# A two-byte shift in place for one of two three-operand instructions in a double-to-float weight conversion

## The chip, the cores and the metric

The kernel runs on one core of one Trainium2 chip. The metric is the device time of one execution in microseconds (us). The profile of one execution is shown beside it. Its engines are TensorE (PE, with its weight loads as PEld), VectorE (DVE), ScalarE (ACT), GpSimd (POOL) and SyncE (SP).

## The reference

Three blocks run one after another, for a batch of 2, 448 tokens and a width of 768:

```
scores = q @ k.T / 8, causal mask, softmax          # 12 heads of 64
x      = (softmax @ v), heads side by side
xk, xr = mu * x + (1 - mu) * x_prev                 # x_prev: the token before
x      = sigmoid(xr @ w_r) * (relu(xk @ w_k)^2 @ w_v)
h      = relu(x @ w_in)
c      = three-tap convolution of h along the tokens
out    = (h * sigmoid(c)) @ w_out
```

The weights `w_r` (768x768), `w_k` and `w_in` (768x1024), `w_v` and `w_out` (1024x768) and the taps `conv_w` reach the kernel as 64-bit floats, the rest as 32-bit floats.

## The kernel before

**Weights.** Each weight matrix is cut into slices: 6 of `w_r` (wr0 to wr5), 8 of `w_k` (wk), 6 of `w_v` (wv), 8 of `w_in` (wi) and 8 of `w_out` (wo). A slice is 128 partitions by 768 values, for wv 128 by 1024. Each is loaded as it is, eight bytes a value, into one of two `wraw` buffers, and `narrow` turns it into 32-bit floats in five steps:

- **a** on ACT: the absolute value of the upper four-byte words, read as floats (they are a double's sign, exponent and first 20 mantissa bits).
- **b** on DVE, or on POOL where the plan says `/p`: clamped to the range that a 32-bit float can hold.
- **c** on DVE: shifted left by 3, with a mask, which moves the exponent and the mantissa to their places.
- **d** on DVE, line 144: sign and top exponent bit are taken from the upper words and put in (three operands: upper words, constant, result so far).
- **e** on DVE, line 146: the top three bits of the lower words are put in as the last mantissa bits (three operands again).

After e the raw buffer is free for the next load. Then ACT makes the high half of a split of the slice (step h, line 87), and DVE or POOL the low half (step l, line 91). TensorE multiplies with both halves, in three passes (`mm3`, line 66). The same five steps run once on a small block of 24 by 128 values, the taps, at the start (`first_steps`).

**Order.** There are three stretches. Attention, the products with `w_r` and the first with `w_k` (up to about 125 us) follow a list written out by hand, `ORDER`, in which each token such as `w3:d` places one step on its engine's queue. The products with `w_k` and `w_v` (to about 238 us) are left to a planner that orders the instructions of each engine by simulated costs. The last stretch, with `w_in`, the convolution and `w_out`, follows a second written list, `LATE`. In each engine's queue instructions run in order. Loads of slices are on SP's queue, each behind step e of the slice that held its buffer.

Of the kernel before, what the change touches and what calls it, by code (L numbers as in the profile page):

```python
# [9 lines left out]
F32 = mybir.dt.float32  # L10
I32 = mybir.dt.int32
I64 = mybir.dt.int64
F32R = mybir.dt.float32r
AF = mybir.ActivationFunctionType
ALU = mybir.AluOpType
# [4 lines left out]
def kernel(  # L20
# [18 lines left out]
    nc = tc.nc  # L39
# [70 lines left out]

    raws = Slots(wp, "wraw", 2, [P, NF * P], I64)
    wcs = Slots(wp, "wc", 2, [P, NF * P])
    whls = Slots(wp, "whl", 4, [P, 2, NF * P], F32R)
    mslots = Slots(mixp, "m", 3, [P, 512])
# [3 lines left out]
    def in_order(ins):  # L118
        if pinned[0]:
            tc.keep_in_program_order(ins)  # L120
# [5 lines left out]
    def as_float(bits):  # L126
        return struct.unpack("<f", struct.pack("<I", bits))[0]

    def as_int(bits):
        return bits - (1 << 32) if bits >> 31 else bits  # L130

    def narrow(step, dst, raw, eng="v"):

        lo, hi = raw[:, 0::2], raw[:, 1::2]
        d = dst.bitcast(I32)
        if step == "a":
            in_order(nc.scalar.activation(dst, hi.bitcast(F32), AF.Abs))
        elif step == "b":
            e = nc.gpsimd if eng == "p" else nc.vector
            e.tensor_scalar(dst, dst, as_float(HIGH), as_float(LOW), ALU.min, ALU.max)  # L140
        elif step == "c":
            nc.vector.tensor_scalar(d, d, 3, as_int(0x3FFFFFF8), ALU.logical_shift_left, ALU.bitwise_and)
        elif step == "d":
            nc.vector.scalar_tensor_tensor(d, hi, as_int(0xC0000000), d, ALU.bitwise_and, ALU.bitwise_or)
        else:
            nc.vector.scalar_tensor_tensor(d, lo, 29, d, ALU.logical_shift_right, ALU.bitwise_or)

    def load(w, m, name, rows, raw=None):

# [17 lines left out]
    def convert(raw, n, name, c=None):  # L167

        c = wcs.turn(f"{name}c") if c is None else c
        for s in "abcde":  # L170
            narrow(s, c[:, :n], raw.bitcast(I32)[:, :2 * n])
        return c
# [30 lines left out]
    def home(tag):  # L203
        return act if tag in early else late[0]

    def big(tag, name):
        return home(tag).tile([P, 2, NT], F32R, tag=tag, name=name)

# [240 lines left out]
    def slot(dtype, name):  # L449
        tag = wo_slots.pop(0)  # L450
        return home(tag).tile([P, 2, WT], dtype, tag=tag, name=name)
# [3 lines left out]
    def first_steps(s):  # L455

        if s == "L":
            t = act.tile([P, 4 * P], F32, tag="U2", name="small")
            small["m"] = mr = t[:2 * NC, :P]
            in_order(nc.sync.dma_start(out=mr[:NC], in_=mu_k.rearrange("(c p) -> c p", p=P)))  # L460
            in_order(nc.sync.dma_start(out=mr[NC:], in_=mu_r.rearrange("(c p) -> c p", p=P)))
            small["r"] = cr = t[:3 * NF, 2 * P:]
            in_order(nc.gpsimd.dma_start(out=cr.bitcast(I64), in_=conv_w.rearrange("t (f p) -> (t f) p", p=P)))
            small["c"] = t[:3 * NF, P:2 * P]
        elif s in "an":
            for x in "a" if s == "a" else "bcde":
                narrow(x, small["c"], small["r"].bitcast(I32))
        elif s == "T":
            pm = bank("small", 1)
            nc.tensor.transpose(pm[:, :2 * NC], small["m"], ident[:2 * NC, :2 * NC])  # L470
            nc.tensor.transpose(pm[:, P:P + 3 * NF], small["c"], ident[:3 * NF, :3 * NF])
        else:
            pm = used("small")
            nc.vector.tensor_copy(mu[:, :2 * NC], pm[:, :2 * NC])
            nc.vector.tensor_scalar(mu[:, 2 * NC:4 * NC], mu[:, :2 * NC], -1.0, 1.0, ALU.mult, ALU.add)
            nc.vector.tensor_copy(cw, pm[:, P:P + 3 * NF])

    class Slice:
# [3 lines left out]
        def step(self, s, eng):  # L482
            e, n = self.e, NC * P
            if s == "L":
                self.raw = raws.get(e, f"{self.name}{self.m}raw")
                load(self.w, self.m, self.name, False, self.raw)
            elif s in "abcde":
                if s == "a":
                    self.c = wcs.get(e, f"{self.name}{self.m}c")
                narrow(s, self.c[:, :n], self.raw.bitcast(I32)[:, :2 * n], eng or "v")  # L490
                if s == "e":
                    raws.put(e)
            elif s == "h":
                self.t = whls.get(e, f"{self.name}{self.m}hl")
                split_h("s", self.t[:, 0, :n], self.c[:, :n])
            else:
                split_l(eng or "v", self.t[:, 1, :n], self.c[:, :n], self.t[:, 0, :n])
                wcs.put(e)
# [143 lines left out]
    def convert_next():  # L642
# [10 lines left out]
        if i < KH:  # L653
            t = slot(F32R, f"b11_{i}")
        wo_c.append(c := convert(*x, slot(F32, f"wo{i}c").rearrange("p a b -> p (a b)")))
# [206 lines left out]
    def pair(name):  # L862
        x = pairs.pop(0)
        if isinstance(x, tuple):
            e, i = x
            if e not in st:
                st[e] = late[0].tile([P, 2, 2, WT], F32R, tag=f"X{e}", name=f"st{e}")
            x = st[e][:, i]
# [195 lines left out]
```

## Time and profile before

| what | value |
|---|---|
| time, median of 3 runs | 354.03 us (353.97 to 354.67) |
| span of the profiled execution | 351.6 us |
| busy PE / DVE / ACT / POOL | 345.2 / 306.9 / 235.1 / 90.3 us |
| granted TensorE clock, mean | 1.000 |

The span runs from the first to the last instruction of the profiled execution; 354.03 - 351.6 = 2.43 us of the median lie around it, and the profiled execution's own time is taken as its span and these 2.43 us. A busy share is an average over the stretches, which have different limits, so what a change is worth is read from who waits for whom.

### The profile page before, as it was taken

The page shows a single profiled execution, that of the slowest core. Times are in us where ns is not written, and L with a number is a line of the kernel's source. Part 1 is how long each engine was busy: PE and PEld are TensorE (multiplying, and loading weights), DVE is VectorE, ACT ScalarE, POOL GpSimd, SP SyncE. Part 2 cuts the span into 40 slices and gives each one's busy share as a digit, 9 for nine tenths or more (in the row PEclk, how much of TensorE's full clock was granted, in tenths as well). Part 3 has the DMA queues.
Part 4 walks back from the last instruction along what each step waited for, and adds up shares of the span by engine and source line. Part 5 has one row for each costly group of instructions (what it writes and reads, how often), then busy time and mean ns, then how long its engine had stood idle before and what let it go on. Part 6 is the DMA issues. An engine that isn't in the chain of part 4 may idle for free.

```text
span 351.6 us, 7196 instructions
## 1 busy us (share of the span) xinstructions
PE 345.2 (98%) x2682; PEld 309.2 (88%) x2682; DVE 306.9 (87%) x629; ACT 235.1 (67%) x515; POOL 90.3 (26%) x149
## 2 busy tenths in 40 slices
PE   7999999999999999999999999999999999999996
PEld 7678788888999998998889999988988999999995
DVE  2999999999889878989999998997998999897741
ACT  2999999999533276767786464354756877766501
POOL 3386986667435000000000000000000000368100
PEclk9999999999999999999999999999999999999999
DMA  5686597442033155347455434543232200379623
GB/s 132 146 222 144 127 222 213 90 116 93 7 95 106 66 180 181 121 148 240 142 187 171 156 101 173 179 143 128 89 103 79 89 2 0 67 134 202 138 91 135
DMA packets 63228, 45.33 MB, mean 129 GB/s; under 512 B 34752, under 2 KB 62156, under 8 KB 63192
## 3 DMA queue, kind: packets, MB, share of 16 engines
q1 hardware_dynamic: 59352, 40.68, 38.7%
q0 software_dynamic: 2912, 3.96, 6.6%
q8 instruction: 21, 0.34, 0.4%
q10 hardware_dynamic: 928, 0.23, 0.3%
q14 instruction: 15, 0.12, 0.1%
HBM read 38.17 MB, written 2.75 MB: 116 GB/s over the span
## 4 chain that ended last, share of the span: by engine, by line
PE 95%; DVE 1%; DMA 1%; POOL 1%; SPq 1%; issue 1%; ACT 0%; POOLq 0%
PE pk L66 17%; PE pv L66 17%; PE pr L66 13%; PE A L66 7%; PE po L391 6%; PE s L321 4%; PE B L66 4%; PE c L66 2%; PE Yb L363 2%; PE D L66 2%; PE Xa L363 2%; PE W L561 1%; PE q L300 1%; PE ph5l L66 1%; PE ph6l L66 1%; PE ph4l L66 1%
## 5 line engine op out<-in xcount | busy, mean ns | idle before, releaser
L887 POOL DMA_DIRECT2D s<-g x12 | 12.7, 1177 | 194.9 <-ACT st L87 188.6
L343 ACT ACTIVATE p<-e,st 128x448 f32<-128x448 f32 (+6 forms) x84 | 42.1, 507 | 1.7 <-DVE st L334 1.5
L72 POOL TENSOR_SCALAR p<-p,st 128x64 f32<-128x64 f32 (+6 forms) x70 | 34.6, 512 | 20.7 <-DVE st L334 11.4
L334 DVE CUSTOM_DVE_ANT_0 e<-s,mask 128x192 f32<-128x192 f32 (+6 forms) x84 | 31.6, 415 | 0.4 <-ACT p L343 0.2
L391 PE MATMUL po<-pt,v 128*64 128x128 f32 (+4 forms) x384 | 24.0, 277 | 0.0
L807 DVE SCALAR_TENSOR_TENSOR cv<-hT,cw,cv 128x448 f32<-128x448 f32 x32 | 21.5, 681 | 2.7 <-ACT cv L804 2.6
L391 PEld LDWEIGHTS po<-pt,v 128*64 128x64 f32 x384 | 20.0, 137 | 3.3 <-issue 0.3
L321 PE MATMUL s<-kT,qT 64*64 64x384 f32 (+6 forms) x336 | 22.1, 386 | 0.5 <-DVE kT L79 0.2
L321 PEld LDWEIGHTS s<-kT,qT 64*64 64x64 f32 x336 | 14.9, 132 | 6.6 <-ACT qT L79 0.7
L343 ACT ACTIVATION_READ_ACCUMULATOR p<-e,st 128x1 f32 x84 | 16.3, 194 | 0.0
L91 POOL TENSOR_TENSOR xr<-m,xr 128x448 fp32r<-128x448 f32 x10 | 12.0, 1198 | 2.1 <-ACT xr L87 1.7
L87 ACT ACTIVATE x<-xv 128x512 fp32r<-128x512 f32 (+1 forms) x12 | 6.8, 573 | 8.1 <-DVE xv L706 8.0
L811 ACT ACTIVATE cv<-cv 128x448 f32<-128x448 f32 x16 | 9.1, 571 | 3.2 <-DVE cv L807 3.2
L999 ACT ACTIVATE o<-A 128x384 f32<-128x384 f32 x3 | 1.5, 491 | 14.7 <-PE A L66 14.6
L804 ACT ACTIVATE cv<-hT,cw 128x448 f32<-128x448 f32 x16 | 10.7, 668 | 0.5 <-DVE g L91 0.3
L813 DVE TENSOR_TENSOR cv<-cv,hT 128x448 f32<-128x448 f32 x16 | 9.9, 621 | 1.2 <-ACT cv L811 1.2
L91 DVE TENSOR_TENSOR k<-a,k 128x512 fp32r<-128x512 f32 (+2 forms) x16 | 9.9, 619 | 0.0
L66 PE MATMUL pv<-k,wv0hl 128*128 128x512 f32 (+1 forms) x48 | 9.9, 364 | 0.0
L66 PE MATMUL pv<-k,wv4hl 128*128 128x512 f32 (+1 forms) x48 | 9.8, 363 | 0.0
L66 PE MATMUL pv<-k,wv2hl 128*128 128x512 f32 (+1 forms) x48 | 9.8, 363 | 0.0
L66 PE MATMUL pv<-k,wv3hl 128*128 128x512 f32 (+1 forms) x48 | 9.8, 363 | 0.0
L66 PE MATMUL pv<-k,wv5hl 128*128 128x512 f32 (+1 forms) x48 | 9.8, 363 | 0.0
(516 smaller groups left out, 1105.0 us busy)
## 6 DMA issues: line engine op xcount, KB each, us to landing
rqk<-in_q_dram SPq DMA_DIRECT2D x24, 112.0 KB, 2.8
rqk<-in_k_dram SPq DMA_DIRECT2D x22, 112.0 KB, 3.0
v<-in_v_dram SPq DMA_DIRECT2D x24, 96.0 KB, 3.0
s<-g POOLq DMA_DIRECT2D x12, 192.0 KB, 3.8
wo6raw<-g POOLq DMA_DIRECT2D x8, 192.0 KB, 4.8
wv0raw<-in_moe_w_v_dram SPq DMA_DIRECT2D x1, 1024.0 KB, 4.8
wv1raw<-in_moe_w_v_dram SPq DMA_DIRECT2D x1, 1024.0 KB, 4.9
wv2raw<-in_moe_w_v_dram SPq DMA_DIRECT2D x1, 1024.0 KB, 5.0
```

The source lines that it names most:

```text
L66: nc.tensor.matmul(ps_out, x, y, start=first and i == 0, stop=last and i == 2, skip_group_check=more,)
L72: nc.gpsimd.tensor_scalar(out_, in_, s, 1.0, ALU.mult, ALU.mult)
L91: e.tensor_tensor(out_, x, f32(h), ALU.subtract)
L321: nc.tensor.matmul(held[self.name(f"s{f}")][1][h, o:z], qT[r, i * LO:(i + 1) * LO], kT[r, :(i + 1) * LO], start=True, stop=True,)
L334: nc.vector.tensor_tensor_reduce(t[:, :w], used(self.name(f"s{f}"))[:, o:z], mask[:, S - w:], -SCALE, 3e38, ALU.add, ALU.min, self.st[:, 0 ...
L343: nc.scalar.activation(p[:, :w], self.s[i][:, :w], AF.Exp, bias=self.st[:, 0, i:i + 1], scale=-1.0, accum_out=self.st[:, 1, i:i + 1],)
L363: nc.tensor.transpose(o[:, u * LO:(u + 1) * LO], self.p[i][r, k0:k0 + P], ident[r, r])
L391: nc.tensor.matmul(self.T["po"][j * D:(j + 1) * D, 1 + i * LO - z:1 + (i + n) * LO], self.v[:, kc, j], self.T["pt"][:, a - z:a + n * LO], ...
L804: nc.scalar.activation(a, x[:, 0:S], AF.Copy, scale=cw[:, f:f + 1])
L807: nc.vector.scalar_tensor_tensor(a, x[:, j:S + j], cw[:, j * NF + f:j * NF + f + 1], a, ALU.mult, ALU.add)
L813: (nc.gpsimd if eng == "p" else nc.vector).tensor_tensor(a, a, hc, ALU.mult)
L887: nc.gpsimd.dma_start(out=dst, in_=f32(x), accum_op=ALU.add)
```

## The change

Steps d and e are rewritten. Step d becomes a two-operand instruction on two-byte elements, inside the raw buffer: it takes the upper half of each lower word (`half[:, 1::4]`), shifts it right by 13, keeps three bits and writes them over the lower half of the upper word (`half[:, 2::4]`), whose bits step a has read before and nobody reads later. Step e becomes the three-operand instruction of the old d with a wider mask, which takes sign, top exponent bit and these three bits at once. The old instruction of e is gone. Tokens and the list order stay.

```
+U16 = mybir.dt.uint16
-        lo, hi = raw[:, 0::2], raw[:, 1::2]
+        hi = raw[:, 1::2]
         d = dst.bitcast(I32)
...
         elif step == "d":
-            nc.vector.scalar_tensor_tensor(d, hi, as_int(0xC0000000), d, ALU.bitwise_and, ALU.bitwise_or)
-        else:
-            nc.vector.scalar_tensor_tensor(d, lo, 29, d, ALU.logical_shift_right, ALU.bitwise_or)
+            half = raw.bitcast(U16)
+            nc.vector.tensor_scalar(half[:, 2::4], half[:, 1::4], 13, 7, ALU.logical_shift_right, ALU.bitwise_and)
+        else:
+            nc.vector.scalar_tensor_tensor(d, hi, as_int(0xC0000007), d, ALU.bitwise_and, ALU.bitwise_or)
```

## Rows read from the trace of the kernel before

**Rows 1.** Busy time by stretch: span, engines with instruction counts, clock, DMA.
```profile
0.00:33.00 33.00, 30.02 (x480) 24.21 (x484) 26.36 (x112) 26.62 (x88) 18.88 (x53) 1.00 0.69 163
33.00:116.00 83.00, 82.96 (x1018) 71.43 (x1011) 79.98 (x202) 65.50 (x174) 54.05 (x76) 1.00 0.46 124
116.00:180.00 64.00, 64.00 (x316) 57.65 (x315) 55.20 (x78) 43.72 (x71) 0.00 (x0) 1.00 0.46 152
180.00:238.00 58.00, 58.00 (x289) 52.12 (x289) 54.61 (x80) 31.38 (x43) 0.00 (x0) 1.00 0.48 158
238.00:300.00 62.00, 62.00 (x311) 55.82 (x310) 57.22 (x97) 44.01 (x90) 0.88 (x1) 1.00 0.21 65
300.00:351.60 51.60, 48.25 (x279) 47.93 (x277) 33.55 (x66) 23.83 (x54) 16.48 (x20) 1.00 0.60 131
sum 351.60, PE 345.23 PEld 309.17 DVE 306.92 ACT 235.06 POOL 90.29; mean PE 57.54 PEld 51.53 DVE 51.15 ACT 39.18 POOL 15.05
```

**Rows 2.** Waits of PE: line, releaser: us in total, times, longest.
```profile
PE W L561 <- POOL ident masks.py:199: 1.7, 1, 1.7
PE Xa L363 <- POOL p L72: 0.2, 1, 0.2
...
PE s L321 <- ACT qT L79: 0.2, 1, 0.2
```

**Rows 3.** Chain that ended last: start us, us, what.
```profile
24.70 0.27 PE Xa L363
...
90.10 30.57 PE pr L66 x147
...
125.00 54.77 PE pk L66 x270
179.77 58.03 PE pv L66 x288
...
348.29 0.49 ACT o L999
```

**Rows 4.** PE in order of time: start, us, line, instruction, count.
```profile
96.32 0.78 PE L66 MATMUL pr<-xr,wr2hl 128*128 128x448 f32 x3
96.94 0.78 PE L66 MATMUL pr<-xr,wr3hl 128*128 128x448 f32 x3
```

**Rows 5.** Step d alone (line 144) by the same stretches: DVE busy.
```profile
33.00:116.00 83.00, 8.21 (x8) 1.00 0.46 124
...
sum 351.60, DVE 36.98; mean DVE 6.16
```

**Rows 6.** Step c alone (line 142) by the same stretches.
```profile
sum 351.60, DVE 21.63; mean DVE 3.61
```

**Rows 7.** Step d's instructions: duration ns min/median/max, first and last start us.
```profile
L144 DVE SCALAR_TENSOR_TENSOR small<-small x1: 280/280/280, 7.3 to 7.3; 24x128 int32<-24x128 int32 x1
L144 DVE SCALAR_TENSOR_TENSOR wr1c<-wr1raw,wr1c x1: 951/951/951, 33.0 to 33.0; 128x768 int32<-128x768 int32 x1
...
L144 DVE SCALAR_TENSOR_TENSOR wk0c<-wk0raw,wk0c x1: 1785/1785/1785, 107.7 to 107.7; 128x768 int32<-128x768 int32 x1
...
L144 DVE SCALAR_TENSOR_TENSOR wv0c<-wv0raw,wv0c x1: 1222/1222/1222, 165.6 to 165.6; 128x1024 int32<-128x1024 int32 x1
```

**Rows 8.** Step c's instructions, same columns.
```profile
L142 DVE TENSOR_SCALAR small<-small x1: 216/216/216, 7.1 to 7.1; 24x128 int32<-24x128 int32 x1
...
L142 DVE TENSOR_SCALAR wk0c<-wk0c x1: 916/916/916, 106.8 to 106.8; 128x768 int32<-128x768 int32 x1
...
L142 DVE TENSOR_SCALAR wk2c<-wk2c x1: 561/561/561, 119.8 to 119.8; 128x768 int32<-128x768 int32 x1
...
L142 DVE TENSOR_SCALAR wv0c<-wv0c x1: 689/689/689, 164.5 to 164.5; 128x1024 int32<-128x1024 int32 x1
```

**Rows 9.** POOL in order of time around wk0's conversion.
```profile
107.27 3.27 POOL L91 TENSOR_TENSOR xk<-mixed,xk 128x448 fp32r<-128x448 f32 x2
```

**Rows 10.** Uses of the split slice wr3: duration ns, first and last start us.
```profile
L66 PE MATMUL pr<-xr,wr3hl x36: 362/368/369, 79.6 to 114.1; 128*128 128x448 f32 x36
...
L91 DVE TENSOR_TENSOR wr3hl<-wr3c,wr3hl x1: 908/908/908, 77.8 to 77.8; 128x768 fp32r<-128x768 f32 x1
```

**Rows 11.** Uses of the split slice wr4, same columns.
```profile
L66 PE MATMUL pr<-xr,wr4hl x36: 368/368/368, 102.5 to 119.7; 128*128 128x448 f32 x36
...
L91 DVE TENSOR_TENSOR wr4hl<-wr4c,wr4hl x1: 958/958/958, 99.9 to 99.9; 128x768 fp32r<-128x768 f32 x1
```

## The prediction, before the changed kernel was run

> **What bounds the kernel now.** I read the busy time by stretch first, because the page's 98% for PE and 87% for DVE leave open which of the two holds up the other. PE is busy for 345.23 of 351.60 us, and what it misses lies at the two ends: 33.00 - 30.02 = 2.98 us before 33 us and 51.60 - 48.25 = 3.35 us after 300 us. Between 33 and 300 us it misses 0.04 us [rows 1]. DVE, on which the changed steps run, is nearly as full up to 116 us (79.98 of 83.00), but it has idle time later.
>
> A busy PE may hide waits, since the ends of matmuls are modelled. So I read three more views. In the waits of PE there are six in all: one of 1.7 us for POOL's identity at the very start and five of 0.2 us, of which the last of the run by time, for POOL's `p`, ends at 24.70 us [rows 2, 3]. In the chain that ended last, everything from 90 us on is matmul pieces in long unbroken runs, 147 of `pr`, 270 of `pk`, 288 of `pv`; the only thing behind PE's last piece is ACT's eviction at 348.29 us and the store [rows 3]. In the order of time three matmuls of 448 columns start every 96.94 - 96.32 = 0.62 us [rows 4]; the same spacing holds through that stretch, whichever slice is used. An engine that waited for DVE would show an uneven spacing. So PE goes at its own pace from 33 us to 348 us, and the time is the start, plus PE's work, plus the tail. The granted clock is 1.00 in every stretch [rows 1], so nothing is to be won or lost there unless PE falls idle.
>
> **What the change does to DVE.** It removes one three-operand instruction per conversion (old e), moves the other one from token d to token e, and adds a two-operand shift at token d. There are 36 slices and the small block, 37 conversions. Both three-operand forms cost the same (951 ns for 768 values, 1222 ns for 1024 [rows 7]; the old e's rows agree with them), so the new e costs what an old one did, and the sum is old d out, new shift in.
>
> The trace has no two-byte instruction with this stride. The nearest row is step c: also one tensor in, two constants, a shift and a mask, result in SBUF, 561 ns for 768 and 689 ns for 1024 values, 216 ns for the small block [rows 8]. It reads 32-bit elements side by side; the shift steps over eight bytes. The old d reads upper words eight bytes apart too, and its rows show what that form of access costs at most, with a second tensor read beside it: 951 ns. Likely value: that of step c. Over all 37 conversions step d takes 36.98 us [rows 5] and step c 21.63 us [rows 6], so DVE's busy time falls by 36.98 - 21.63 = 15.35 us, to about 291.6 us. Bounds: if the strided shift goes at the old d's pace, the fall is 0; if it is as slow as the slowest old d, 1785 ns [rows 7], each one costs 0.83 us more than 0.95, and DVE's busy time rises by 36 x 0.83 = 30 us.
>
> [...]
>
> **What of it reaches the time.** Before 33 us there is one conversion whose d is changed, the small block at 7.3 us: 280 - 216 = 64 ns earlier [rows 7, 8]. DVE's next work there waits for PE and ACT within a few us, so I take 0, with 0.06 us as the other end. The first large d, wr1's, starts at 33.0 us [rows 7], after the last wait of PE. From there on a DVE that finishes earlier gives PE an operand earlier that PE was not waiting for. What hides DVE's saving is PE's own queue, full to 348 us. So the 15.35 us go into idle time of DVE, and into earlier starts of ACT's step h and of the loads that stand on SP's queue behind step e. These loads feed step a of slices that PE needs later; none is on the chain. Token d no longer needs step c's result, only that step a has read the raw words, which c's own place behind a already assures; on DVE's in-order queue nothing is held longer. The raw buffer is written by DVE now, but its next load waits for step e as before.
>
> Sum: 351.60 + 2.43 = 354.03, less 0 to 0.06 us. I predict 354.0 us. Within 0.2%, 0.71 us, is about what a measurement of this kernel cannot tell from no change; its three runs lie 0.70 us apart.
>
> **Rivals.**
>
> *A slow shift makes PE wait (slower).* The place is the hand-ordered stretch before 116 us, where DVE has 83.00 - 79.98 = 3.0 us idle [rows 1]. The tightest slice I found is wr3: DVE's low half starts at 77.8 us and takes 0.91, ending at 78.7, and PE's first use is at 79.6 [rows 10], a margin of 0.9 us. Four shifts stand before it (wr1, wr2, wr0, wr3). It decides from 0.9 / 4 = 0.23 us above the old d on, that is a shift of 1.18 us. At 1785 ns the four put it 4 x 0.83 = 3.3 us later, PE waits about 3.3 - 0.9 = 2.4 us, and wr4 adds 0.83 us less its margin of 102.5 - 100.9 = 1.6 [rows 11], which that wait has widened already. The time would be about 356.4 us. For it: an unmeasured form of access. Against it: the old d reads at the same distance and takes no longer for it than 951 ns.
>
> *The shift and POOL block each other (slower or nothing).* At wk0, step c took 916 ns in place of 561, and the old d 1785 in place of 951, while POOL worked on `xk` [rows 8, 7, 9]. A blocked shift like that c costs 0.92 us, still under the usual old d; so on DVE this gives no loss, and on POOL a shorter holder than before. If each of the seven shifts between 33 and 116 us were held up by one POOL instruction of 3.27 / 2 = 1.6 us [rows 9], a shift would take 0.56 + 1.6 = 2.2 us, past the point above, and the four before wr3 would cost 4 x 1.2 - 0.9 = 4 us: 358 us. POOL is busy for 54.05 of 83.00 us there, yet only that one of the seven old d's in that stretch was held so long [rows 1, 5], which speaks against it. [...]
>
> *A new plan of the middle stretch (slower).* Between 125 and 238 us the order comes from simulated costs, and another cost for d can reorder DVE's queue. If one conversion step were put ahead of an operand that PE needs next, PE would wait for at most about that step, 1.22 us [rows 7]: 355.2 us. Against it: DVE is idle there for 64.00 - 55.20 + 58.00 - 54.61 = 12 us [rows 1] and gets more, and PE's queue has no gap that shows a thin margin.
>
> *DVE bound PE after all (faster).* If half of the saving between 33 and 116 us, where DVE is fullest, reached PE, that would be half of 8.21 - 8 x 0.56 = 3.7 us [rows 5, 8], so 352.2 us. Against it: PE's even spacing and the missing waits.
>
> *The shift gains nothing on DVE.* Then DVE's busy time stays near 307 us and the time at 354.0: the same time as my forecast by another way.
>
> **How the numbers follow.** Forecast with the saving hidden, 0.70, and with no saving, 0.09: both within 0.2%. Slow shift 0.05, POOL 0.02, new plan 0.06: slower, 0.13 together, though 1 in 10 of a new plan may cost too little to be told. Faster, 0.08. So faster 0.08, same 0.79, slower 0.13. The range takes all that is within 0.2% (353.3 to 354.7) and, above, most of the new plan's cases, to 355.1; left out are the slow shift, POOL's case and the faster case, together 0.15, and the edge.
>
> **What the profile after would show.** Line 144 as a two-operand instruction of about 560 ns for 768 and 690 for 1024 values, 21 to 22 us in all; DVE's busy time near 292 us; PE's at 345 us with no new wait after 25 us; `pr` still at 0.62 us for three. The prediction is wrong if PE shows waits for line 91 or for POOL after 33 us, if the shift is above 1.18 us, or if PE's work between 33 and 348 us takes less time than now.

## The result, and the profile after

| | before | changed |
|---|---|---|
| time, median | 354.15 us (353.97 to 354.67, 4 runs) | 357.56 us (356.35 to 359.52, 4 runs) |
| span of the profiled execution | 351.6 us | 355.3 us (its time 357.05) |

The ratio is 1.0101, 95% interval 1.0067 to 1.0134: slower by 1%, where no change was forecast and the range ended at 355.1 us. The single runs also lie 3.2 us apart instead of 0.7.

The busy time by stretch, the answer to [rows 1] (the first three stretches have PE's busy time as before):

```profile
...
180.00:238.00 58.00, 56.37 (x277) 49.79 (x276) 47.56 (x70) 28.03 (x38) 0.00 (x0) 1.00 0.42 137
238.00:300.00 62.00, 61.40 (x305) 54.58 (x304) 58.18 (x98) 43.18 (x85) 0.00 (x0) 1.00 0.22 73
...
sum 355.30, PE 346.57 PEld 309.13 DVE 306.28 ACT 234.71 POOL 90.66; mean PE 57.76 PEld 51.52 DVE 51.05 ACT 39.12 POOL 15.11
```

PE was full from 33 to 300 us. Now it misses 1.63 us between 180 and 238 us and 0.60 us from there to 300 us. DVE's busy time is nearly what it was, 306.28 against 306.92 us; of the 15.35 us that it should have lost, 0.64 us are there. The shift's rows, which answer to [rows 7], say why (duration in ns, then first and last start):

```profile
...
L146 DVE TENSOR_SCALAR wr1raw<-wr1raw x1: 1035/1035/1035, 33.2 to 33.2; 128x768 uint16<-128x768 uint16 x1
...
L146 DVE TENSOR_SCALAR wk0raw<-wk0raw x1: 1991/1991/1991, 107.9 to 107.9; 128x768 uint16<-128x768 uint16 x1
...
```

A shift takes 1035 ns, more than the three-operand instruction that it replaced (951). All 37 together take 40.71 us where step d took 36.98 [rows 5]. In DVE's queue the two differ less than by their durations, because the next instruction starts before the recorded end of the one ahead of it. An old d and what follows it in the kernel before, then a shift and what follows it in the changed kernel (start, us):

```profile
206.81 0.95 DVE L144 SCALAR_TENSOR_TENSOR wo3c<-wo3raw,wo3c 128x768 int32<-128x768 int32 x1
207.68 0.68 DVE L91 TENSOR_TENSOR x<-xv,x 128x512 fp32r<-128x512 f32 x1
```

```profile
204.09 1.05 DVE L146 TENSOR_SCALAR wi0raw<-wi0raw 128x768 uint16<-128x768 uint16 x1
204.93 0.73 DVE L92 TENSOR_TENSOR x<-xv,x 128x512 fp32r<-128x512 f32 x1
```

The old d holds the queue for 0.87 us and the shift for 0.84; that is why dearer shifts leave the busy time where it was. A shift of 1.04 us is also below the 1.18 us from which the prediction let it reach PE. PE's new waits, which answer to [rows 2], do not lie where a slow shift would have put them, before 116 us:

```profile
PE pv L67 <- ACT k L88: 0.9, 1, 0.9
PE pv L67 <- DVE k L92: 0.8, 1, 0.8
PE ph0l L67 <- ACT x L88: 0.4, 1, 0.4
...
PE ph0l L67 <- DVE x L92: 0.2, 1, 0.2
```

They lie at two places of the planner's stretch and its end. At the first (190 to 192 us) the last half tile of the squared activations `k` comes late for `pv`: its rounding on ACT stood ahead of a step of wo2, a table load (1.28 us), `sr` and wv4's step a in the kernel before, and stands behind them now (the kernel before, then the changed kernel):

```profile
182.91 0.53 ACT L87 ACTIVATE k<-a 128x384 fp32r<-128x384 f32 x1
```

```profile
189.51 0.52 ACT L88 ACTIVATE k<-a 128x384 fp32r<-128x384 f32 x1
```

At the second (244 us) the product `x` comes late for `ph0l`, the first products of the last stretch. The last matmul of `pv` starts at 239.9 us (237.5 before), the last of `ph0l` at 245.2 (241.5): 2.4 us are gone at the end of `pv`, 3.7 at the end of `ph0l`, and 355.3 - 351.6 = 3.7 is what the span grew by. PE's idle time in these waits is only 2.23 us. Most of the rest stands in its busy time, which grew by 346.57 - 345.23 = 1.34 us: a matmul that stands alone behind a wait is listed with 0.45 or 0.50 us, where 18 in one run take 4.28.

The chain that ended last was PE for 95% of the span. Now the page has this:

```profile
PE 59%; DVE 17%; DMA 14%; ACT 5%; issue 2%; POOL 1%; SPq 1%; ACTq 0%; POOLq 0%
```

And piece by piece (start, us, what), the second half of the planner's stretch, which was `pv` in one run [rows 3]:

```profile
198.09 4.50 DMA wi0raw<-in_moe_w_in_dram
...
211.02 0.97 DVE wo3c L148
212.04 5.57 DMA wi1raw<-in_moe_w_in_dram
217.69 0.90 ACT wi1c L138
...
221.87 0.88 DVE wi1c L148
222.81 4.45 DMA wi2raw<-in_moe_w_in_dram
...
234.66 0.96 DVE wi3c L148
235.62 0.61 DVE xv L708
...
239.48 0.79 ACT wi4c L138
...
244.06 0.70 DVE x L92
244.81 0.73 PE ph0l L67 x2
```

This chain holds no `pv` matmul between 198 and 244 us. It reads: load of a slice, its conversion, the next load into the buffer that the conversion frees, and the evictions `xv` and `x` in between, behind conversion steps on DVE's queue. At first I took the two waits of PE for two separate losses; the experiments corrected that.

One more thing had changed that the diff does not name. Compared instruction by instruction, 81 places of ACT's queue, 124 of DVE's, 5 of PE's and 2 of SP's hold another instruction than before, all in the planner's stretch. The hand-ordered stretches are untouched.

### The profile page after: what moved, and what is told of

Same layout as the page of the kernel before. It is cut to its first block, busy times and chain, and to the rows that moved or that the text cites. A ratio compares the mean times of both kernels' runs of the same rounds, so it can differ in the third digit from the quotient of the medians.

```text
span 355.3 us, 7160 instructions
## 1 busy us (share of the span) xinstructions
PE 346.6 (98%) x2682; PEld 309.1 (87%) x2682; DVE 306.3 (86%) x629; ACT 234.7 (66%) x515; POOL 90.7 (26%) x149
## 4 chain that ended last, share of the span: by engine, by line
PE 59%; DVE 17%; DMA 14%; ACT 5%; issue 2%; POOL 1%; SPq 1%; ACTq 0%; POOLq 0%
PE pr L67 12%; PE A L67 7%; PE po L393 6%; PE s L323 4%; PE B L67 4%; PE c L67 2%; PE Yb L365 2%; PE D L67 2%; PE Xa L365 2%; DMA wv5raw<-in_moe_w_v_dram 2%; DMA wi1raw<-in_moe_w_in_dram 2%; PE W L563 1%; DMA wv1raw<-in_moe_w_v_dram 1%; DMA wv3raw<-in_moe_w_v_dram 1%; PE q L302 1%
## 5 line engine op out<-in xcount | busy, mean ns | idle before, releaser
L67 PEld LDWEIGHTS pv<-k,wv0hl 128*128 128x128 f32 x48 | 8.6, 188 | 3.4 <-ACT k L88 1.3
L67 PE MATMUL pv<-k,wv1hl 128*128 128x512 f32 (+1 forms) x48 | 10.0, 363 | 0.0
```

Source lines behind the costliest of these rows:

```text
L67: nc.tensor.matmul(ps_out, x, y, start=first and i == 0, stop=last and i == 2, skip_group_check=more,)
```

## The experiments

In most of them the planner's order is replaced by a list, one for each of ACT, DVE, PE and SP, over the middle and last stretch. No wait is taken away by it.

```diff
+    for seq in PINS.values():
+        seq = ["I-" + n for n in seq.split()]
+        for x, y in zip(seq, seq[1:]):
+            tc.add_manual_dep(
+                by[y], x, mybir.DependencyInfo(mybir.DependencyClass.NoSync, mybir.DependencyReason.DATA), reason="pin",
+            )
```

| run | instructions and order | median, us (runs) | ratio, 95% interval |
|---|---|---|---|
| e1 | changed steps, order of the kernel before | 354.49 (10) | 1.0002, 0.999 to 1.0013 |
| e2 | old steps, order of the changed kernel | 360.67 (4) | 1.0179, 1.0152 to 1.0206 |
| e3 | changed steps, shift held behind c, planned anew | 360.55 (4) | 1.0181, 1.0142 to 1.022 |
| e5 | changed steps, new order up to wi0 | 358.41 (4) | 1.0109, 1.0076 to 1.0142 |
| e6 | changed steps, new order from wi0 on | 361.11 (4) | 1.0198, 1.0179 to 1.0217 |
| e7 | changed kernel, two halves of `k` earlier | 359.10 (4) | 1.0135, 1.012 to 1.015 |
| e8 | e7 and five instructions of x[4] earlier | 357.81 (4) | 1.0124, 1.0051 to 1.0197 |
| e9 | e6 with two loads swapped | 355.92 (4) | 1.0043, 1.0028 to 1.0058 |
| e10 | e7, wi0 converted behind wo3, loads swapped | 354.32 (10) | 1.0003, 0.9982 to 1.0023 |
| e11 | e5 and the two halves of `k` earlier | 354.64 (10) | 1.0009, 0.9994 to 1.0024 |

**Is it the order or the instructions?**

> The changed kernel's instructions, but on every engine in the order in which the kernel before was planned (a forced order for the middle and last stretch). Theory A, the plan: the 3.4 us come from the new order that the planner made of DVE's and ACT's queues; then this run is near the kernel before, 354.0 to 354.9 us, with no wait of PE above 0.3 us after 125 us. Theory B, the price: the shift takes 1.04 us where step d took 0.95, and the ring of two raw buffers (load, steps a to e, next load) is stretched until PE waits, whatever the order; then 356.3 us or more.

> The instructions of the kernel before, but on every engine in the order that the planner made for the changed kernel (where that order has the shift ahead of step c, old c and d stand there in this order, since old d needs c). Theory A, the plan: 356.3 us or more, with waits of PE for k2 and x2 near 185 and 240 us. Theory B, the price: 353.9 to 354.9 us, since the prices are the old ones.

> The changed kernel, where the planner must leave each shift behind step c of its slice, as the old step d was; all else is the planner's. Theory A: if it was the shift's freedom to go ahead of c that changed the plan, 354.0 to 354.9 us; if the order comes out other than before all the same, anything up to 358. Theory B: 356.3 us or more.

The edit of e3, apart from the lists:

```diff
-            nc.vector.tensor_scalar(half[:, 2::4], half[:, 1::4], 13, 7, ALU.logical_shift_right, ALU.bitwise_and)
+            s = nc.vector.tensor_scalar(half[:, 2::4], half[:, 1::4], 13, 7, ALU.logical_shift_right, ALU.bitwise_and)
+            if not pinned[0]:
+                tc.add_manual_dep(
+                    s.ins, last_c[0].ins.name,
...
+                )
```

With the order of before, the changed steps take the time of before (e1), although each shift costs 1.04 us: PE shows no wait over 0.2 us after 25 us. With the order of the changed kernel, the old steps are slow, with one wait of 3.7 us at `pv` (e2; where the new order has the shift ahead of c, the old c and d change places, 20 of 37 times). So the order costs the 1%, and the shift's price no time. e3 puts the shift behind c as the old d was; the planner then finds yet another order, also slow, with one wait of 3.8 us at `ph0l`. So the shift's freedom to go ahead of c is not needed for the loss.

**What does a shift cost, and why?**

> The changed kernel with step d in seven forms in turn, one slice each, to measure prices: two-byte with step 4 in place (as changed), 32-bit with step 2 in place, two-byte side by side, two-byte with step 2, 32-bit side by side, two-byte step 4 into side by side, side by side into step 4. The results of the conversion are other numbers than the reference's; only durations are read. If two-byte elements with a step are what is slow: about 1.04 us for every two-byte form with a step and about 0.56 us for the 32-bit forms at 768 values. If any step is slow: about 1.0 us for the 32-bit form with step 2 too. Two-byte side by side: 0.56 us or less.

The edit takes one of seven forms in turn (in most of them the shifted bits end up elsewhere, so the weights are other numbers):

```diff
+            out_, in_ = (
+                (half[:, 2::4], half[:, 1::4]),
+                (raw[:, 1::2], raw[:, 0::2]),
+                (half[:, 0:n], half[:, n:2 * n]),
+                (half[:, 0:2 * n:2], half[:, 1:2 * n:2]),
+                (word[:, 0:n], word[:, n:2 * n]),
+                (low[:, 0:n], half[:, 1::4]),
+                (half[:, 2::4], low[:, 0:n]),
+            )[form]
+            nc.vector.tensor_scalar(out_, in_, 13, 7, ALU.logical_shift_right, ALU.bitwise_and)
```

One instruction of each form, in the order of the list (duration in ns):

```profile
L161 DVE TENSOR_SCALAR wk6raw<-wk6raw x1: 1059/1059/1059, 147.3 to 147.3; 128x768 uint16<-128x768 uint16 x1
...
L161 DVE TENSOR_SCALAR wr1raw<-wr1raw x1: 560/560/560, 34.0 to 34.0; 128x768 int32<-128x768 int32 x1
L161 DVE TENSOR_SCALAR wr2raw<-wr2raw x1: 356/356/356, 57.1 to 57.1; 128x768 uint16<-128x768 uint16 x1
L161 DVE TENSOR_SCALAR wr0raw<-wr0raw x1: 604/604/604, 70.9 to 70.9; 128x768 uint16<-128x768 uint16 x1
L161 DVE TENSOR_SCALAR wr3raw<-wr3raw x1: 557/557/557, 73.4 to 73.4; 128x768 int32<-128x768 int32 x1
L161 DVE TENSOR_SCALAR wr4c<-wr4raw x1: 548/548/548, 91.7 to 91.7; 128x768 uint16<-128x768 uint16 x1
L161 DVE TENSOR_SCALAR wr5raw<-wr5c x1: 1046/1046/1046, 100.3 to 100.3; 128x768 uint16<-128x768 uint16 x1
```

The last two rows separate it. Reading two-byte elements at a step of 4 and writing them side by side costs 548 ns; reading side by side and writing at a step of 4 costs 1046. It is the scattered two-byte write that takes the time. Four-byte elements at a step of 2 lie just as far apart and cost 560, as side by side (557).

**Where in the order does it cost?** At this point I held a theory of two places: each of PE's waits is a loss of its own, about 2.1 and 1.3 us, and they add up.

> The changed kernel's instructions. ACT, DVE and PE keep the changed kernel's order up to the conversion of wi0 (about 210 us); from there on, and on SP's loads of wi1 and wo4, the order is that of the kernel before. Two-places theory: the loss at the first place (PE waiting for the two halves of k2's last tile, about 190 to 192 us) stays, the loss at the second (ph0l waiting for x, about 240 to 245 us) goes: 356.0 to 356.6 us, PE waits of about 1.6 us at pv and none at ph0l. Rival, the loss belongs to the second place alone: 354.2 to 354.8 us. Rival, what goes wrong at the second place is the late work of the first handed on: no less than the changed kernel, 357 us or more, with ph0l still waiting.

> The changed kernel's instructions, the order of the kernel before up to the conversion of wi0, and the changed kernel's order after that (ACT, DVE, and SP's two loads). Two-places theory: no wait at pv, ph0l still waits for x: 355.1 to 355.8 us. Rival, the first place alone costs: 354.2 to 354.8 us. Rival, the second place costs as much as both together: 356.5 us or more.

> The changed kernel in its own order but for two instructions: the rounding of k2's last half tile goes ahead of the rounding of wo2c, sr2's sigmoid and wv4's step a on ACT, and the subtraction behind it goes ahead of wv4's step b on DVE. Two-places theory: these two queue places are the whole of the first loss: 1.6 to 2.1 us less than the changed kernel, 355.4 to 356.0 us, no wait of PE at pv, and the waits at ph0l stay. Rival, the first loss comes from ACT and DVE having too much in front of pv whatever the order there: the wait turns up at pv's next tiles and the time stays at 356.8 us or more.

> As the run with the two halves earlier, and five more instructions moved: x[4]'s eviction, product and halves on DVE go ahead of steps of wi2's and wi3's conversions, and x[4]'s first rounding on ACT goes ahead of wi3's step a. Two-places theory: queue order at the two places is all that costs: 354.2 to 355.0 us, no PE wait over 0.3 us after 25 us, though some 140 instructions on ACT and DVE still stand elsewhere than in the kernel before. Rival, the order of the rest matters too, or SP's changed load of wo4 ahead of wi1 holds the second place by itself: 355.3 us or more, with ph0l waiting for x.

The edits are moves in the lists. For e7 (on ACT, and on DVE) and for e8 also the five of x[4]:

```diff
 ACT: ... relu, square of k's last half
+     k[7] high half
      b<-wo2c, sr2, wv4 step a
-     k[7] high half
 DVE: ... b<-wo2c
+     k[7] low half
      wv4 step b, wv4 shift
-     k[7] low half
```

The theory of two separate losses fell. e5's profiled execution was as expected (356.44 us, 1.7 us of waits at `pv`, none at `ph0l`), but its median, 358.41 us, was not. e6, with the new order at the second place alone, was slower than the whole new order. And e7, which took the first wait away, won nothing: PE came to `ph0l` 1.5 us earlier (238.64 us for the changed kernel's 240.11), found `x` not there, and waited longer, as PE's rows in order of time show:

```profile
238.64 3.60 PE L149 MATMUL ph0l<-x,wi0hl 128*128 128x512 f32 x15
245.05 1.95 PE L149 MATMUL ph0l<-x,wi0hl 128*128 128x512 f32 x3 [2.81 <-ACT x L170]
246.80 1.48 PE L149 MATMUL ph1l<-x,wi1hl 128*128 128x512 f32 x3
```

So `x` comes at about 244 to 245 us by its own chain, whatever happens at `pv`. The wait cost more than itself. The three matmuls of `ph1l` took 1.48 us, in the changed kernel 0.85. The busy time of PE in stretches of 5 us, with the granted clock behind it, says why:

```profile
240.00:245.00 5.00, 2.25 (x10) 1.00 0.08 30
245.00:250.00 5.00, 4.95 (x16) 0.66 0.12 25
```

After the wait of 2.8 us the granted clock was 0.66 in this stretch; against 1.00 that is 5 x 0.34 = 1.7 us of work (an estimate). Wait and clock, 2.8 + 1.7 = 4.5 us, make up most of the 357.5 - 352.4 = 5.1 us by which e7's span exceeds that of e10. The changed kernel's own waits, 0.9 us and less, left the clock at 1.00. The profiles of e2, e3 and e8, with one PE wait of 3.7, 3.8 and 2.5 us, show such a stretch too (lowest 0.77, 0.70 and 0.73), and e6 one of 0.66 behind a wait of 2.0 us; these runs were slower than the changed kernel. e5's three slower runs list a mean clock of 0.995, its profiled one 1.0; by these figures 0.005 x 357 = 1.8 us of work are lost (an estimate), most of the 2 to 3 us by which they exceed the profiled one. Whether and where they waited no profile shows.

e8 moved x[4] ahead by 6 us (its first eviction from 235.53 to 229.46 us), and x[5], which PE waits for, came as late as ever, at 244.46 us. Moving x[4] did not help; x[5]'s own place was not moved, and what came late was in front of it.

**What makes x late?** The loads, and x[5]'s place behind them. SP's queue in the kernel before, then in the changed kernel (start, us, line, destination):

```profile
198.62 0.34 SPq L159 DMA_DIRECT2D wo3raw<-in_moe_w_out_dram  x1
203.69 0.37 SPq L159 DMA_DIRECT2D wi0raw<-in_moe_w_in_dram  x1
209.30 0.37 SPq L159 DMA_DIRECT2D wi1raw<-in_moe_w_in_dram  x1
214.05 0.34 SPq L159 DMA_DIRECT2D wo4raw<-in_moe_w_out_dram  x1
```

```profile
195.76 0.34 SPq L161 DMA_DIRECT2D wo3raw<-in_moe_w_out_dram  x1
198.09 0.37 SPq L161 DMA_DIRECT2D wi0raw<-in_moe_w_in_dram  x1
207.17 0.34 SPq L161 DMA_DIRECT2D wo4raw<-in_moe_w_out_dram  x1
212.04 0.37 SPq L161 DMA_DIRECT2D wi1raw<-in_moe_w_in_dram  x1
```

Before, a load goes out about every 5 us, and each slice is converted in the order of the loads. In the changed order wo3 is loaded first but converted after wi0: its raw buffer is taken from 195.8 to 212.0 us, and then wo4, whose conversion stands behind wi1's, takes the other. There are two raw buffers. So the load of wi1 goes out at 212.0 us in place of 209.3, wi2's at 222.8 in place of 219.8, and all the evictions between the steps of these conversions in DVE's queue move with them. In e6, where wo3 is converted first, SP's queue alone does the same: wi1's buffer was free at 212.1 us, but its load stood behind wo4's, which waited for wi0's buffer:

```profile
214.99 0.34 SPq L243 DMA_DIRECT2D wo4raw<-in_moe_w_out_dram  x1
215.38 0.43 SPq L243 DMA_DIRECT2D wi1raw<-in_moe_w_in_dram  x1
```

> As e6 (the changed kernel's instructions, its own order from the conversion of wi0 on), but SP issues the load of wi1 ahead of that of wo4 again: two places of one queue differ from e6, whose loads of wo4 and wi1 went out together at 215.0 and 215.4 us although wi1's buffer was free at 212.2. Loads theory: the order of ACT and DVE from wi0 on costs little, e6's loss is the load of wi1 standing behind that of wo4: the load of wi1 at 212 to 212.5 us, wi1's step a at about 217, no PE wait over 0.3 us at ph0l or one below 1, 354.3 to 355.8 us. Rival, ACT's and DVE's places from wi0 on cost by themselves: PE still waits 2 us or more at ph0l, 357.5 us or more.

> As e7 (the changed kernel's own order with k2's last two halves ahead), and wi0's conversion steps a to e put behind wo3's on ACT and DVE, with the loads in the order wi1, wo4: the buffer that wo3 holds from 195.8 to 211.0 us in the changed kernel is given back earlier. x[4] and x[5] stay where the changed kernel's order has them. Loads theory: wo3's last step ends at about 208 us, the load of wi1 goes out at 208 to 209.5 (212.0 in the changed kernel), x's last half comes at 242 us or before, and PE waits less than 0.5 us at ph0l: 354.2 to 355.2 us. Rival, evictions standing behind the conversions in DVE's queue hold ph0l whenever the loads come: x's last half at 244 us or later, PE waits 2 us or more, 357.5 us or more.

> As e5 (the changed kernel's order up to wi0, the order of the kernel before from there), with the two halves of k2's last tile moved ahead as in e7. If these two places in ACT's and DVE's queues are the whole of the first loss: no PE wait at pv and none at ph0l, 354.0 to 354.8 us, though more than 100 instructions on ACT and DVE still stand elsewhere than in the kernel before. Rival, the late conversions of the first part hold something later: 355.3 us or more, with a PE wait that e5 did not show.

```diff
 e9, SP:
-     load wo4, load wi1
+     load wi1, load wo4
 e10, ACT and DVE, besides e7's moves and e9's:
-     wi0 steps a to e, wo3 steps a to e
+     wo3 steps a to e, wi0 steps a to e
```

Two places on SP's queue took e6 from 361.11 to 355.92 us (e9). The load of wi1 went out at 210.8 us, 1.2 us earlier than expected, as this execution's loads ran ahead of e6's from wo3 on (200.1 for 201.5 us); the wait at `ph0l` fell from 3.8 us to 0.2 in the profiled run, which at 354.93 us is its fastest. The median is 0.1 us above what I expected, and 0.4% over the kernel before stay with the rest of that order. e10 keeps x[4] and x[5] where the changed kernel has them, converts wo3 first, and is at 1.0003. Its load of wi1 went out at 210.0 us, half a microsecond later than expected, and x[5]'s first half came at 241.2 + 0.7 = 241.9 us, just as PE came to it:

```profile
210.03 0.37 SPq L243 DMA_DIRECT2D wi1raw<-in_moe_w_in_dram  x1
```

e10 changes the order of the conversions and of the two loads at once. By the rows, the first is what counts in the changed kernel, where wo4's load had gone out 5 us before wi1's buffer came free; neither was run alone.

Late loads alone do not make PE wait, though. The load of wi4 and x[5]'s first half, in the kernel before, the changed kernel, e1 (whose load is shown with its duration in ns, then its start) and e10:

```profile
229.33 0.37 SPq L159 DMA_DIRECT2D wi4raw<-in_moe_w_in_dram  x1
237.66 0.68 DVE L91 TENSOR_TENSOR x<-xv,x 128x512 fp32r<-128x512 f32 x1
```

```profile
232.42 0.37 SPq L161 DMA_DIRECT2D wi4raw<-in_moe_w_in_dram  x1
244.06 0.69 DVE L92 TENSOR_TENSOR x<-xv,x 128x512 fp32r<-128x512 f32 x1 [0.70 <-ACT x L88]
```

```profile
L243 SPq DMA_DIRECT2D wi4raw<-in_moe_w_in_dram x1: 367/367/367, 232.5 to 232.5; - x1
240.99 0.72 DVE L174 TENSOR_TENSOR x<-xv,x 128x512 fp32r<-128x512 f32 x1
```

```profile
229.56 0.37 SPq L243 DMA_DIRECT2D wi4raw<-in_moe_w_in_dram  x1
241.21 0.69 DVE L174 TENSOR_TENSOR x<-xv,x 128x512 fp32r<-128x512 f32 x1 [0.70 <-ACT x L170]
```

In e1's profiled execution the load is as late as in the changed kernel, but in the old order x[5] ends 9.2 us behind it (9.0 in the kernel before). In the new order it ends 12.3 us behind it, in the changed kernel and in e10, because wi4's step a on ACT and the eviction of x[5] on DVE stand further back; in e10 the load is in time. Both e1 and e10 bring x[5] at 241.7 to 241.9 us, when PE needs it. So each of the two delays, about 3 us, uses up the margin without a loss, and only together, in the changed kernel and e7, do they make PE wait. Why e1's loads ran late in the old order is open: e6 and e9, with the same order up to wi0, load wo3 at 201.5 and 200.1 us, e1 at 202.1.

e11 closes the first place: with the two halves earlier and the old order from wi0 on, 1.0009 and no wait at either place, though more than a hundred instructions stand elsewhere than before.

## Why the prediction was wrong

- **PE at its own pace from 33 to 348 us.** Right for the kernel before, and the measure of the loss: the span grew by what PE lost up to `pv` and `ph0l`. (What lies around the span was taken as 2.43 us; it is 357.05 - 355.3 = 1.75.)
- **The shift's price, the term of the sum.** Mis-sized: step c's 561 ns was taken, 1035 was measured; by its durations DVE's step d became 3.73 us dearer in all instead of 15.35 us cheaper, and DVE's busy time fell by 0.64 us. It was inside the bounds (1785 ns) and cost no time (e1). The choice of step c as the nearest row rested on the instruction's form and passed over the write: no row of before writes two-byte elements scattered. In e4 the read at a step of 4 kept step c's pace (548 ns) and the write did not (1046).
- **"What hides DVE's saving is PE's own queue".** The saving did not exist, so this was not tried. A step d of 1.04 us in place of 0.95 did stay hidden, before 116 us in the changed kernel and everywhere in e1, but in DVE's queue it was hardly dearer; wr3's low half started at 78.2 us instead of 77.8, still ahead of PE's first use.
- **The new plan, 0.06.** This is the step that failed. The mechanism was named among the rivals, but priced as one conversion step put ahead of one operand, 1.22 us at most, and the sum took nothing for it. At the first place several instructions were put ahead of `k`, and 2.4 us were lost. At the second a chain came: a conversion out of the order of the loads, a raw buffer held for 16 us, the next load late, with it the conversions and evictions behind it on ACT and DVE, and x[5]'s eviction 3 us further back among them. Where SP's queue alone makes wi1's load late, in e6, the loss is 6.8 us, as the clock was 0.66 behind a wait of PE of 2.0 us there, too. In the changed kernel the loss is 3.4 us with both places, since the first wait had already delayed PE and the second was short.
- **What spoke against the new plan did not bear on it.** DVE's 12 us of idle time are no cover for a queue in order: in the changed kernel DVE idles for 3.53 us before wi1's step b and the evictions stand behind it. And a full PE shows no margin, neither thick nor thin. The margin was in the rows of the kernel before: x[5]'s first half ended at 237.66 + 0.68 = 238.3 us; the 16th of `ph0l`'s 18 matmuls, which starts between 237.6 and 241.5, needs it at about 237.6 + 15 x 3.9 / 17 = 241.0. A margin of 2.7 us (an estimate from these rows) is about half the distance between two loads, and less than the two delays of about 3 us together.
- **POOL's block and DVE as the bound.** Neither came, but for wk0's shift: it took 1991 ns beside POOL's two instructions on `xk` (107.56 to 110.77 us), as its old d had taken 1785; the other shifts of 768 values took 1029 to 1083. (The prediction counts seven old d's between 33 and 116 us; the row has eight.)

Open is what in the planner tips: the shift's simulated price, its other operands, or the dependency of e on it. e3 shows only that its freedom to go ahead of c is not needed. A third raw buffer, which would uncouple the loads from the conversions, was not tried. Nor was an execution of the changed kernel above 359 us seen in a profile, so what widened its runs to 3.2 us is open; all four list a mean clock of 1.0.

## What to carry to other kernels

Where a planner orders part of a kernel, changing the price or form of one instruction changes the program: compare the order of every queue, SP's too, before the new time is put down to the instruction, and run the new instructions in the old order. With few load buffers, the order of conversions and the order of loads have to agree (here, with two, one buffer was held for 16 us); read the distance between loads and the time that each buffer is held, and compare the margin of the next operand with one load. And when a wait is taken away and the time does not fall, look for the chain that arrives behind it: here the chain that ended last named it from the start.

## What was not expected of the hardware

A two-byte write at a step of four elements took 1029 to 1083 ns for 768 values in the changed kernel and e4 (but for wk0's, 1991 and 1999), nearly twice the two-byte read at that step written side by side in e4 (548 and 561) and three times the form that is side by side on both sides (350 to 356). Yet in the rows shown the next instruction on DVE started 0.84 us after such a shift, against 0.87 us after a three-operand instruction of 949 ns. Four-byte elements at a step of 2 cost no more in e4 than side by side (548 to 560 against 549 to 557). A step of 2 on both sides cost 604 to 618 for two-byte elements.

In e7 a wait of PE of 2.8 us was followed by a granted clock of 0.66 over the next 5 us, in which three matmuls took 1.48 us instead of 0.85; the changed kernel's two waits of 0.8 and 0.9 us left it at 1.00.
